# Planner costs taken from a trace, jittered filler priorities, and a later product with beta in a fused attention and gated-MLP kernel

## The chip, the core and the metric

The kernel runs on one core of a Trainium2 chip. The metric is device time in microseconds (us) of one execution, as the median of repeated runs. Below, PE is the matrix engine (TensorE; PEld is its weight load), DVE the vector engine, ACT the scalar engine, POOL the GpSimd engine, SP the engine that issues most DMAs.

## The reference

One layer over 2048 tokens of width 512 in bf16. Two branches read the same input `x`, and a gate mixes them:

```python
g = sigmoid((x * gate_w).sum(-1, keepdims=True))
a = A(x)     # attention with a compressive memory
b = B(x)     # gated MLP
return g * a + (1 - g) * b
# A: 32 heads of 16, four segments s of 512 tokens, q, k, v = x @ wq, wk, wv
p = softmax(q_s @ k_s.T * 16**-0.5 + mask)        # mask: keys up to the query
a_mem = (phi(q_s) @ M) / (phi(q_s) @ z + 1e-6)    # phi(t) = t + 1 if t > 0 else exp(t)
o_s = sigmoid(beta) * a_mem + (1 - sigmoid(beta)) * (p @ v_s)
M, z = M + phi(k_s).T @ v_s, z + phi(k_s).sum()   # then the next segment
a = o @ wo
# B: h = gelu(x @ w_gate) * (x @ w_up)  (512 -> 1792);  b = h @ w_down
```

## The kernel before

**The planner.** The kernel's body doesn't issue instructions in the order in which it is written. It describes the work as tasks (`Task`, line 43). A task has an engine or a choice of engines, a length in ns that the author states, a priority (lower goes first), dependences, and buffers that it takes and frees. Among those are the eight banks of PSUM, the memory that PE writes. `Sched.plan` (line 74) plays these tasks through in time with the stated lengths: whenever an engine is free, it starts that one of its ready tasks with the lowest priority number. The result is one fixed list, and `emit` (line 267) issues it. On the chip each engine works through its own instructions strictly in that order and waits by semaphores. The stated lengths thus never change what is computed. They set the order in which each engine gets its work, and which of two engines gets a task that either could do. If a task takes longer on the chip than stated, whatever the plan placed behind it stands and waits, even if other work would be ready.

**Stages.** First come the loads, the transposes of the first segment's `x`, and the products for k, q and v of segment 0. Then comes a gate stage: 28 tasks (`gate_pair`, line 618), each of 32 matmuls into two banks, which ACT turns into gelu and writes to `G`. Between the gate tasks of segments 0 and 1 stands one small product with `beta` (`f_bps`, line 643, priority -942). From it ACT and DVE make `omg` and `ebr`, the weights of the two attention halves; `ebr` goes into `bdeb` (`f_eb`, line 651), and `wo` is scaled by `omg` (`f_wo`, line 657). Tasks of this stage have negative priorities, so they go in the written order.

**The attention stage.** It has 80 logit slots, 20 per segment (`logit_slot`, line 694). A slot is a small PE product, two exponentials of 128x1024 on ACT (line 735), and two mask operations on POOL (line 744). PE can't be filled by these: between the slots run fillers, which `fillers` (line 1006) lists per segment, with priorities that count in slots. They are the up-projections (`up_group`, line 631, result multiplied into `G` by DVE), the q, k, v products of the next segment, the memory products (`mem_den`, `mem_num`, `m_update`), and the output products (`out_group`, line 973: down-projection and `wo` into one bank). After every five slots come two products of the probabilities with v (`pv_group`, line 752) and a chain on DVE: transpose `T` (line 781), reciprocal `r` (791), `r` times the gate (794), `N` from `T` and `r` (799), plus the memory part `Nm` (804), transpose into `xT` (807). `Nm` comes from line 952. `phi` (line 820) is one exponential on ACT, a maximum and a minimum on DVE (829, 832), and an addition on POOL (836). The output products of the last segment come at the end.

**Where the lengths stand.** `EV` (line 435) holds the default length of a task that empties a bank (`evac`, line 437); other lengths are literals in the `add` calls.

Of the kernel before, what the change touches and what calls it, by code (L numbers as in the profile page):

```python
# [1 line left out]

# [22 lines left out]
HS = DFF // P  # L25
# [8 lines left out]
SLACK = 300  # L34
NWARM = 7
NUPS = (28, 10, 9, 9)
SHAPES = {"gen": [(b,) for b in range(NBANK)],
          "pair": [(b, b + 1) for b in range(NBANK - 1)]}
WIDTH = {k: len(v[0]) for k, v in SHAPES.items()}
# [14 lines left out]
class Sched:  # L54
# [7 lines left out]
    def __init__(self, rings):  # L62
        self.tasks = []
        self.bufs = rings

    def add(self, engs, cost, fn, **kw):

        engs = {engs: cost} if isinstance(engs, str) else dict(zip(engs, cost))
        t = Task(engs, fn, **kw)
        t.seq = len(self.tasks)  # L70
        self.tasks.append(t)
        return t
# [199 lines left out]
def kernel(  # L272
# [36 lines left out]
    add = S.add  # L309
# [122 lines left out]
                **kw)  # L432
        return t, box

    EV = {"DVE": 610, "ACT": 560}

    def evac(engs, g, box, fn, prio=0.0, deps=(), alloc=(), frees=(), ring="gen", cost=None):
        engs = [engs] if isinstance(engs, str) else engs
# [29 lines left out]
    def odd_copy(s, c, ev):  # L468
        pr = c // 2
        ko = ("o", s, pr)  # L470

        def fo(e):
            if ko not in QK:
                QK[ko] = rtile("kO", [P, 2, L])
            nc.vector.tensor_scalar_mul(QK[ko][:, c % 2, :], QK[("k", s, pr)][:, c % 2, :],
                                        odd[:, :])
        new = ko not in first_ev
        o = add("DVE", 400, fo, prio=2, deps=[ev] + ([] if new else [first_ev[ko]]),
                alloc=["kO"] if new else [])
        first_ev.setdefault(ko, o)  # L480
        EVQK[("o", s, c)] = o
# [136 lines left out]
    def gate_pair(s, hp, prio):  # L618
        def mms(t):
            for i in range(2):  # L620
                mm_x(t[:, i, :], wga, (2 * hp + i) * P, s)
        g, box = group("gt", 8 * MM, mms, prio, [a_x[s], a_wg0 if hp < 2 else a_wga], alloc="pair")
        read_x[s].append(g)
        dst = G[:, s, 2 * hp:2 * hp + 2, :]
        ge = evac("ACT", g, box, lambda e, t: nc.scalar.activation(dst, t[:, :, :],  # L625
                                                                  AF.Gelu_apprx_tanh),
                  cost=960, ring="pair")
        GM[(s, hp)] = ge
        TAB["last_gt"], TAB["last_ge"] = g, ge

# [35 lines left out]
    for s in range(NSEG):  # L666
        if s == 3:
            gate_rows(-960 + 20 * s)
        for hp in range(HS // 2):
            gate_pair(s, hp, -959 + 20 * s + hp)  # L670
            if s == 0 and hp == HS // 2 - 1:
                g, box = group("bps", 60, f_bps, -942, [a_be])
                t_tb = evac("ACT", g, box, lambda e, t: nc.scalar.activation(
                    tb[:, :], t[:, 0:NCH], AF.Tanh, scale=0.5), cost=250)
                t_om = add("DVE", 100, f_omg, deps=[t_tb], prio=5)
                t_eb = add("DVE", 1200, f_eb, deps=[t_om], prio=5)
                t_wo = add("DVE", 1300, f_wo, deps=[t_om, a_wo], prio=7)
# [16 lines left out]
    def logit_slot(s, t):  # L694
# [37 lines left out]
        for h in range(2):  # L732
            def fx(_, h=h):
                pT[(s, t, h)] = rtile("pT", [P, 2, L])
                nc.scalar.activation(pT[(s, t, h)][:, :, :], A[h][:, :, :], AF.Exp, scale=0.25)  # L735

            def fa(_, h=h):
                pt = pT[(s, t, h)]
                if w in (0, 3):
                    v, pat = pt[:, :, 0:P], [[0, 2], [1, P]]  # L740
                else:
                    v = pt[:, :, :].rearrange("p h (e c) -> p (h e) c", e=2)[:, :, 0:P]
                    pat = [[0, 4], [1, P]]
                nc.gpsimd.affine_select(out=v, in_=v, pattern=pat, compare_op=ALU.is_ge,  # L744
                                        fill=0.0, base=0, channel_multiplier=-1)
            x = add("ACT", 920 + (1300 if gi == 0 and h == 0 else 0), fx, prio=1,
                    deps=[g, TAB["last_ge"]] + ([XT_[(gi, 0)]] if h else []), alloc=["pT"],
                    frees=[(("pair", h), g)])
            XT_[(gi, h)] = x
            AT[(gi, h)] = add("POOL", 380 if w in (0, 3) else 610, fa, prio=0, deps=[x])  # L750

    def pv_group(s, c, e):
        g0 = s * NSLOT + 5 * c
# [25 lines left out]

        def f_T(_, t):  # L780
            nc.vector.transpose(TT[key][:, e, :, :].rearrange("p a b -> p (a b)"), t[:, :])  # L781
        ev = evac("DVE", g, box, f_T)
        if e == 0:
            NMT[("T", key)] = g
            NMT[("Te", key)] = ev
# [20 lines left out]
        def f_o(_):  # L806
            nc.vector.transpose(xT[:, c, s * L:(s + 1) * L],
                                NN[key][:, :, :, :].rearrange("p a e d -> p (a e d)"))
        r = add("DVE", 280, f_r, prio=3, deps=[ev, NMT[("Te", key)]], alloc=["r"])
        rg = add("DVE", 120, f_rg, prio=3, deps=[r, TAB["g2"]])  # L810
        n = add("DVE", 650, f_n, prio=3, deps=[rg], alloc=["N"], frees=[("r", r), ("T", T0)])
        last = n
        if s > 0:
            last = add("DVE", 500, f_m, prio=3, deps=[n, NMT[("Nm", key)]],
                       frees=[("Nm", NMT[("Nm", key)])])
        OTT[key] = add("DVE", 640, f_o, prio=3, deps=[last] + read_x[s], frees=[("N", n)])

    PQ, PKt, PHI, PKD, RMt = {}, {}, {}, {}, {}

    def phi(src, deps, prio, mk, ring):  # L820
        box = {}

        def f_e(_):
            box["E"] = rtile("E", [P, 2, L])
            nc.scalar.activation(box["E"][:, :, :], src()[:, :, :], AF.Exp)

        def f_q(_):
            box["Q"] = rtile("Q1", [P, 2, L])
            nc.vector.tensor_scalar_max(box["Q"][:, :, :], src()[:, :, :], 0.0)

        def f_m(_):
            nc.vector.tensor_scalar_min(box["E"][:, :, :], box["E"][:, :, :], 1.0)

        def f_a(_):
            d = mk()
            nc.gpsimd.tensor_add(d[:, :, :], box["E"][:, :, :], box["Q"][:, :, :])
        e = add("ACT", 980, f_e, prio=prio, deps=deps + [TAB["first_x"], opened], alloc=["E"])
        q = add("DVE", 380, f_q, prio=5, deps=[e], alloc=["Q1"])
        m = add("DVE", 380, f_m, prio=5, deps=[e])
        return add("POOL", 2250, f_a, prio=5, deps=[m, q], alloc=[ring],  # L840
                   frees=[("E", e), ("Q1", q)])

    def phi_q(s, pr, prio):
# [22 lines left out]
    def m_update(s, pr, prio):  # L866
# [31 lines left out]
                bd[:, :, 0].rearrange("p (j e) -> p j e", j=4)[:, None, :, :]  # L898
                .to_broadcast((P, NCH, 4, 2)))
        deps = [TAB[("acc", s, 0)], acc, t_eb] + [TAB[("num", s, c)] for c in range(NCH) if s]  # L900
        TAB[("mbd", s)] = add("DVE", 620, f_mbd, prio=3, deps=deps)
        TAB[("zbd", s)] = add("DVE", 150, f_zbd, prio=3, deps=deps + ([TAB[("den", s)]] if s else []))

    def mem_den(s, prio):
        bx = {}
# [22 lines left out]
            nc.vector.tensor_mul(RMt[s][:, :, :], RMt[s][:, :, :],  # L928
                                 G2[:, s, :][:, :, None].to_broadcast((P, QB, 8)))
        ev = evac("DVE", g, box, f_T)  # L930
        a = add("DVE", 200, f_a, prio=2, deps=[ev], alloc=["rm"], frees=[("Tm", g)])
        r = add("DVE", 880, f_r, prio=2, deps=[a])
        TAB[("rm", s)] = add("DVE", 250, f_g, prio=2, deps=[r])
        TAB[("rma", s)] = a

    def mem_num(s, c, prio):
# [13 lines left out]
        def f_n(_):  # L950
# [2 lines left out]
                                 RMt[s][:, :, 2 * c:2 * c + 2][:, :, :, None]  # L953
                                 .to_broadcast((P, QB, 2, DH)))
        ev = evac("DVE", g, box, f_T)
        NMT[("Nm", (s, c))] = add("DVE", 680, f_n, prio=2.5, deps=[ev, TAB[("rm", s)]],
                                  alloc=["Nm"], frees=[("Tm", g), ("rm", TAB[("rma", s)])])

    def down(t, s, qt, lo, hi, stop):
# [13 lines left out]
    def out_group(s, qt, prio):  # L973


        late = s == NSEG - 1
        att = [t_wo] + [OTT[(s, c)] for c in range(NCH)]
        prev = first = None
        for lo in range(0, HS, 2):
            def fn(_, lo=lo):  # L980
                down(bank(first), s, qt, lo, lo + 2, False)
            prev = add("PE", 2 * MM, fn, prio=prio, mode="more" if lo else "open",
                       deps=[prev] if lo else [UPT[(s, hs)] for hs in range(HS)] + [TAB["wdn"]]
                       + ([] if late else att), alloc=[] if lo else ["gen"], final=late)
            first = first or prev
        g = add("PE", 4 * MM, lambda _: proj_o(bank(first), s, qt, range(NCH), False),
                prio=prio, deps=[prev] + att, final=late, mode="more")
        bx = {}

        def fo(e):  # L990
            bx["o"] = rtile("osb", [P, D])
            f = omz[:, s, qt:qt + 1]
            if e == "ACT":
                nc.scalar.activation(bx["o"][:, :], bank(first), AF.Copy, scale=f)  # L994
            else:
                nc.vector.tensor_scalar_mul(bx["o"][:, :], bank(first), f)  # L996
        ev = add(["DVE", "ACT"], [670, 590], fo, deps=[g, TAB["omz"]], alloc=["osb"],
                 frees=[("gen", first)])
        add("SP", 600, lambda _: store(s, qt, bx["o"]), deps=[ev], frees=[("osb", ev)], lat=2000)

# [78 lines left out]
```

## Time and profile before

| what | us |
|---|---|
| median of three runs (282.32, 282.30, 283.60) | 282.32 |
| the profiled execution, its own time | 284.42 |
| its span, first to last instruction | 282.7 |
| PE busy in the span | 272.1 |
| ACT busy | 211.3 |
| DVE busy | 173.2 |
| POOL busy | 129.1 |

The profiled execution is 1.7 us longer than its span (what lies around the program), and 2.1 us longer than the median run. Busy times are unions of recorded instructions. Records on PE, ACT and DVE overlap their successors a little: two exponentials in a row, 1025 ns each by the group's mean, take 1.94 us together, so one costs 0.92 us when ACT is kept supplied. In a window's row, each engine's busy us stands with its number of instructions in brackets, followed by the PE clock that was granted as a share of full speed, and DMA. In a row of waits stand the waiting engine and line, the one that ended the wait, and then us in total, times, and longest us.

### The profile page before, as it was taken

The page shows a single profiled execution, that of the slowest core. Times are in us where ns is not written, and L with a number is a line of the kernel's source. Part 1 is how long each engine was busy: PE and PEld are TensorE (multiplying, and loading weights), DVE is VectorE, ACT ScalarE, POOL GpSimd, SP SyncE. Part 2 cuts the span into 40 slices and gives each one's busy share as a digit, 9 for nine tenths or more (in the row PEclk, how much of TensorE's full clock was granted, in tenths as well). Part 3 has the DMA queues.
Part 4 walks back from the last instruction along what each step waited for, and adds up shares of the span by engine and source line. Part 5 has one row for each costly group of instructions (what it writes and reads, how often), then busy time and mean ns, then how long its engine had stood idle before and what let it go on. Part 6 is the DMA issues. An engine that isn't in the chain of part 4 may idle for free.

```text
span 282.7 us, 10149 instructions
## 1 busy us (share of the span) xinstructions
PE 272.1 (96%) x4498; PEld 126.6 (45%) x4504; DVE 173.2 (61%) x316; ACT 211.3 (75%) x231; POOL 129.1 (46%) x220
## 2 busy tenths in 40 slices
PE   8999899999999989999999999999999998999994
PEld 3444344444445444454445445444444443444541
DVE  2330210102879898989897797999758699535330
ACT  3545466457897777999898898898889889798520
POOL 8000000060565376486857477457645756444400
PEclk9999999999999999999999999999999998999999
DMA  7963970000022010020010020000000000000011
GB/s 237 345 125 77 339 252 2 0 0 2 3 42 39 2 39 2 2 42 2 21 39 22 3 58 23 3 2 2 21 21 22 2 21 3 21 21 21 23 38 39
DMA packets 22036, 14.02 MB, mean 50 GB/s; under 512 B 14056, under 2 KB 20968, under 8 KB 21992
## 3 DMA queue, kind: packets, MB, share of 16 engines
q1 hardware_dynamic: 21448, 12.85, 16.0%
q8 instruction: 35, 0.57, 0.9%
q10 hardware_dynamic: 544, 0.52, 0.6%
q14 instruction: 9, 0.07, 0.1%
HBM read 8.13 MB, written 2.10 MB: 36 GB/s over the span
## 4 chain that ended last, share of the span: by engine, by line
PE 74%; DVE 8%; SPq 7%; ACT 4%; DMA 2%; issue 2%; POOL 0%; ACTq 0%; DVEq 0%
PE ps L461 48%; PE ps L457 13%; PE ps L713 8%; SPq L360 7%; PE ps L763 5%; ACT pT L735 3%; DMA wdn<-in_A_x_dram 1%; DVE N L799 1%; DVE G L635 1%; DVE vz_82 L299 1%; DMA beta_76<-in_A_beta_dram 1%; DVE r L794 1%; DVE T L781 1%; DVE Nm L952 1%; DVE N L804 1%
## 5 line engine op out<-in xcount | busy, mean ns | idle before, releaser
L735 ACT ACTIVATE pT<-ps 128x1024 bf16<-128x1024 f32 x160 | 153.9, 1025 | 20.9 <-PE ps L713 20.2
L744 POOL TENSOR_SCALAR_AFFINE_SELECT pT<-pT 128x512 bf16<-128x512 bf16 (+1 forms) x160 | 92.5, 586 | 83.1 <-ACT pT L735 82.6
L461 PE MATMUL ps<-wdn,G 128*32 128x512 bf16 x896 | 59.3, 386 | 0.5 <-ACT pT L735 0.5
L461 PE MATMUL ps<-xT,wup 128*32 128x512 bf16 x896 | 55.2, 380 | 0.9 <-DVE G L635 0.8
L635 DVE TENSOR_TENSOR G<-ps,G 128x512 bf16<-128x512 f32 x56 | 37.6, 678 | 20.7 <-PE ps L461 20.3
L457 PE MATMUL ps<-xT,wga 128*128 128x512 bf16 x219 | 48.4, 379 | 0.4 <-issue 0.2
L625 ACT ACTIVATE G<-ps 128x1024 bf16<-128x1024 f32 x28 | 28.7, 1025 | 24.2 <-PE ps L457 23.5
L457 PEld LDWEIGHTS <-wga 128*128 128x128 bf16 x224 | 21.8, 98 | 26.4 <-issue 0.4
L461 PEld LDWEIGHTS <-wup 128*32 128x32 bf16 x896 | 22.3, 96 | 22.9 <-issue 4.7
L461 PEld LDWEIGHTS <-G 128*32 128x32 bf16 x896 | 21.9, 97 | 21.3 <-issue 3.9
L781 DVE STREAM_TRANSPOSE T<-ps 128x512 f32<-128x512 f32 x32 | 22.7, 708 | 13.6 <-PE ps L763 13.4
L596 POOL COPY G_87<-tt 32x16 f32<-32x16 f32 x16 | 3.1, 195 | 49.3 <-DVE tt L588 48.6
L713 PE MATMUL ps<-qT,kT 16*128 16x256 bf16 (+2 forms) x320 | 17.9, 273 | 1.5 <-DVE vz_82 L299 1.2
L713 PE MATMUL ps<-qT,kO 32*128 32x128 bf16 (+2 forms) x320 | 18.5, 276 | 0.1
L461 PEld LDWEIGHTS <-xT 128*32 128x32 bf16 x448 | 11.4, 96 | 11.3 <-issue 1.6
L461 PE MATMUL ps<-wo,xT 128*32 128x512 bf16 x256 | 16.5, 379 | 0.0
L713 PEld LDWEIGHTS <-kT 16*128 16x128 bf16 x320 | 6.9, 92 | 19.4 <-issue 19.1
L799 DVE TENSOR_TENSOR N<-T,r 128x512 bf16<-128x512 f32 x16 | 14.2, 887 | 0.4
L713 PEld LDWEIGHTS <-kO 32*128 32x128 bf16 x320 | 7.1, 93 | 14.8 <-issue 14.6
L994 ACT ACTIVATE osb<-ps,omz 128x512 bf16<-128x512 f32 x6 | 4.1, 687 | 11.5 <-PE ps L461 11.5
L996 DVE TENSOR_SCALAR osb<-ps,omz 128x512 bf16<-128x512 f32 x10 | 7.4, 743 | 8.6 <-PE ps L461 8.5
L461 PE MATMUL ps<-xT,wk 128*32 128x512 bf16 x192 | 12.5, 380 | 0.0
(116 smaller groups left out, 282.1 us busy)
## 6 DMA issues: line engine op xcount, KB each, us to landing
out_dram<-osb SPq DMA_DIRECT2D x16, 128.0 KB, 1.7
wup<-in_B_w_up_dram SPq DMA_DIRECT2D x1, 1792.0 KB, 8.1
wdn<-in_B_w_down_dram SPq DMA_DIRECT2D x1, 1792.0 KB, 13.5
wga<-in_B_w_gate_dram SPq DMA_DIRECT2D x1, 1280.0 KB, 10.3
wq<-in_A_wq_dram SPq DMA_DIRECT2D x1, 512.0 KB, 6.0
wga<-in_B_w_gate_dram SPq DMA_DIRECT2D x1, 512.0 KB
wv<-in_A_wv_dram SPq DMA_DIRECT2D x1, 512.0 KB, 7.9
wo<-in_A_wo_dram SPq DMA_DIRECT2D x1, 512.0 KB, 9.1
```

The source lines that it names most:

```text
L360: nc.sync.dma_start_transpose(xT[:, fc, s * L:(s + 1) * L], x2[s * L:(s + 1) * L, fc * P:(fc + 1) * P])
L457: nc.tensor.matmul(t, lhsT=lhsT, rhs=rhs, start=start, stop=stop)
L461: nc.tensor.matmul(t[a, :], lhsT=lhsT[:, a], rhs=rhs, start=start, stop=stop, tile_position=(0, 32 * j), skip_group_check=True)
L625: ge = evac("ACT", g, box, lambda e, t: nc.scalar.activation(dst, t[:, :, :], AF.Gelu_apprx_tanh), cost=960, ring="pair")
L635: UPT[(s, hs)] = evac("DVE", g, box, lambda e, t: nc.vector.tensor_mul(G[:, s, hs, :], t[:, :], G[:, s, hs, :]))
L713: nc.tensor.matmul(A[j // 2][:, j % 2, at * P:(at + nq) * P], lhsT=l, rhs=r, start=True, stop=True, tile_position=(32 * j, 0))
L735: nc.scalar.activation(pT[(s, t, h)][:, :, :], A[h][:, :, :], AF.Exp, scale=0.25)
L744: nc.gpsimd.affine_select(out=v, in_=v, pattern=pat, compare_op=ALU.is_ge, fill=0.0, base=0, channel_multiplier=-1)
L763: nc.tensor.matmul(t[32 * j:32 * j + 32, qb * P:(qb + nq) * P], lhsT=vz[s % 2][:, kt, h * VW:h * VW + 32], rhs=pT[(s, t0 + w, j // 2)][:, ...
L781: nc.vector.transpose(TT[key][:, e, :, :].rearrange("p a b -> p (a b)"), t[:, :])
L799: nc.vector.tensor_mul(NN[key][:, :, :, :].rearrange("p a e d -> p e a d"), TT[key][:, :, :, 0:DH], RR[key][:, :, :, :].to_broadcast((P, 2 ...
L996: nc.vector.tensor_scalar_mul(bx["o"][:, :], bank(first), f)
```

## The change

It has four parts. Nothing is computed differently.

1. 24 stated lengths are altered. The largest steps: `N` 650 to 800, `r` times gate 120 to 245, `Nm` 680 to 765, `Mbd` 620 to 825, `zbd` 150 to 335, `odd_copy` 400 to 320, the POOL addition 2250 to 2090, an ACT evacuation 560 to 495, gelu 960 to 920.
2. In `add`, every task that can only run on PE and has a priority above 0 and below 9000 gets a random number between -1.5 and 1.5 added to it, from a generator with a fixed seed. This covers all fillers. Logit slots (-10), `pv_group` (-9), the gate stage (negative) and the last segment's output products (9000 and up) are outside it.
3. The product with `beta` goes from behind the gate tasks of segment 0 to behind those of segment 1 (priority -942 to -922).
4. `out_group` waits for `att[:ATT]` with `ATT = 5`. The list `att` has five members (`t_wo` and four of `OTT`), so this is the same list.

```diff
+ATT = 5
+SEED = 7
+SPREAD = 1.5
@@ Sched.__init__, Sched.add
+        self.rng = Random(SEED)
+        if "PE" in engs and 0 < kw["prio"] < 9000:
+            kw["prio"] += self.rng.uniform(-SPREAD, SPREAD)
@@ evac's default lengths; odd_copy; gate_pair
-    EV = {"DVE": 610, "ACT": 560}
+    EV = {"DVE": 605, "ACT": 495}
-        o = add("DVE", 400, fo, prio=2, ...
+        o = add("DVE", 320, fo, prio=2, ...
-                  cost=960, ring="pair")
+                  cost=920, ring="pair")
@@ the gate stage
-            if s == 0 and hp == HS // 2 - 1:
-                g, box = group("bps", 60, f_bps, -942, [a_be])
+            if s == 1 and hp == HS // 2 - 1:
+                g, box = group("bps", 60, f_bps, -922, [a_be])
@@ logit_slot (masks), pv_group (T, r, r x gate, N, + Nm, to xT)
-            AT[(gi, h)] = add("POOL", 380 if w in (0, 3) else 610, fa, ...
+            AT[(gi, h)] = add("POOL", 400 if w in (0, 3) else 635, fa, ...
-        ev = evac("DVE", g, box, f_T)
+        ev = evac("DVE", g, box, f_T, cost=625)
-        r = add("DVE", 280, f_r, ...       rg 120   n 650   m 500   o 640
+        r = add("DVE", 260, f_r, ...       rg 245   n 800   m 490   o 610
@@ phi (e, q, m, POOL addition)
-        980, 380, 380, 2250
+        960, 330, 345, 2090
@@ m_update (Mbd, zbd), mem_den (a, r, g), mem_num (Nm)
-        620, 150;   200, 880, 250;   680
+        825, 335;   120, 860, 285;   765
@@ out_group
-                       + ([] if late else att), ...
+                       + ([] if late else att[:ATT]), ...
-        ev = add(["DVE", "ACT"], [670, 590], fo, ...
+        ev = add(["DVE", "ACT"], [660, 585], fo, ...
```

More of the change, by code (lines that the diff above doesn't have):

```diff
@@ L1 @@
 from contextlib import ExitStack
+from random import Random
 import concourse.bass as bass
@@ L477, in odd_copy @@
         new = ko not in first_ev
-        o = add("DVE", 400, fo, prio=2, deps=[ev] + ([] if new else [first_ev[ko]]),
+        o = add("DVE", 320, fo, prio=2, deps=[ev] + ([] if new else [first_ev[ko]]),
                 alloc=["kO"] if new else [])
@@ L749, in logit_slot @@
             XT_[(gi, h)] = x
-            AT[(gi, h)] = add("POOL", 380 if w in (0, 3) else 610, fa, prio=0, deps=[x])
+            AT[(gi, h)] = add("POOL", 400 if w in (0, 3) else 635, fa, prio=0, deps=[x])
     def pv_group(s, c, e):
@@ L808, in f_o @@
                                 NN[key][:, :, :, :].rearrange("p a e d -> p (a e d)"))
-        r = add("DVE", 280, f_r, prio=3, deps=[ev, NMT[("Te", key)]], alloc=["r"])
-        rg = add("DVE", 120, f_rg, prio=3, deps=[r, TAB["g2"]])
-        n = add("DVE", 650, f_n, prio=3, deps=[rg], alloc=["N"], frees=[("r", r), ("T", T0)])
+        r = add("DVE", 260, f_r, prio=3, deps=[ev, NMT[("Te", key)]], alloc=["r"])
+        rg = add("DVE", 245, f_rg, prio=3, deps=[r, TAB["g2"]])
+        n = add("DVE", 800, f_n, prio=3, deps=[rg], alloc=["N"], frees=[("r", r), ("T", T0)])
         last = n
         if s > 0:
-            last = add("DVE", 500, f_m, prio=3, deps=[n, NMT[("Nm", key)]],
+            last = add("DVE", 490, f_m, prio=3, deps=[n, NMT[("Nm", key)]],
                        frees=[("Nm", NMT[("Nm", key)])])
-        OTT[key] = add("DVE", 640, f_o, prio=3, deps=[last] + read_x[s], frees=[("N", n)])
+        OTT[key] = add("DVE", 610, f_o, prio=3, deps=[last] + read_x[s], frees=[("N", n)])
     PQ, PKt, PHI, PKD, RMt = {}, {}, {}, {}, {}
@@ L836, in f_a @@
             nc.gpsimd.tensor_add(d[:, :, :], box["E"][:, :, :], box["Q"][:, :, :])
[L837 to L840, printed above, removed]
+        e = add("ACT", 960, f_e, prio=prio, deps=deps + [TAB["first_x"], opened], alloc=["E"])
+        q = add("DVE", 330, f_q, prio=5, deps=[e], alloc=["Q1"])
+        m = add("DVE", 345, f_m, prio=5, deps=[e])
+        return add("POOL", 2090, f_a, prio=5, deps=[m, q], alloc=[ring],
                    frees=[("E", e), ("Q1", q)])
@@ L900, in m_update @@
         deps = [TAB[("acc", s, 0)], acc, t_eb] + [TAB[("num", s, c)] for c in range(NCH) if s]
-        TAB[("mbd", s)] = add("DVE", 620, f_mbd, prio=3, deps=deps)
-        TAB[("zbd", s)] = add("DVE", 150, f_zbd, prio=3, deps=deps + ([TAB[("den", s)]] if s else []))
+        TAB[("mbd", s)] = add("DVE", 825, f_mbd, prio=3, deps=deps)
+        TAB[("zbd", s)] = add("DVE", 335, f_zbd, prio=3, deps=deps + ([TAB[("den", s)]] if s else []))
     def mem_den(s, prio):
@@ L930, in mem_den @@
         ev = evac("DVE", g, box, f_T)
-        a = add("DVE", 200, f_a, prio=2, deps=[ev], alloc=["rm"], frees=[("Tm", g)])
-        r = add("DVE", 880, f_r, prio=2, deps=[a])
-        TAB[("rm", s)] = add("DVE", 250, f_g, prio=2, deps=[r])
+        a = add("DVE", 120, f_a, prio=2, deps=[ev], alloc=["rm"], frees=[("Tm", g)])
+        r = add("DVE", 860, f_r, prio=2, deps=[a])
+        TAB[("rm", s)] = add("DVE", 285, f_g, prio=2, deps=[r])
         TAB[("rma", s)] = a
@@ L955, in mem_num @@
         ev = evac("DVE", g, box, f_T)
-        NMT[("Nm", (s, c))] = add("DVE", 680, f_n, prio=2.5, deps=[ev, TAB[("rm", s)]],
+        NMT[("Nm", (s, c))] = add("DVE", 765, f_n, prio=2.5, deps=[ev, TAB[("rm", s)]],
                                   alloc=["Nm"], frees=[("Tm", g), ("rm", TAB[("rma", s)])])
@@ L983, in out_group @@
                        deps=[prev] if lo else [UPT[(s, hs)] for hs in range(HS)] + [TAB["wdn"]]
-                       + ([] if late else att), alloc=[] if lo else ["gen"], final=late)
+                       + ([] if late else att[:ATT]), alloc=[] if lo else ["gen"], final=late)
             first = first or prev
@@ L996, in fo @@
                 nc.vector.tensor_scalar_mul(bx["o"][:, :], bank(first), f)
-        ev = add(["DVE", "ACT"], [670, 590], fo, deps=[g, TAB["omz"]], alloc=["osb"],
+        ev = add(["DVE", "ACT"], [660, 585], fo, deps=[g, TAB["omz"]], alloc=["osb"],
                  frees=[("gen", first)])
```

## The prediction

> **What bounds the kernel.** I first read the busy shares, then the busy time by stage, then PE's waits, then the stretches around them. PE is busy in 96% of the span, and in the attention stage (some 66 to 263 us) in all but a few us. What is left to win is therefore PE's idle time, not any engine's load.
>
> ```profile
> PE 272.1 (96%) x4498; PEld 126.6 (45%) x4504; DVE 173.2 (61%) x316; ACT 211.3 (75%) x231; POOL 129.1 (46%) x220
> ```
> ```profile
> 90.00:120.00 30.00, 28.81 (x588) 13.59 (x584) 26.28 (x46) 23.90 (x27) 15.71 (x23) 1.00 0.05 11
> ...
> 150.00:180.00 30.00, 29.19 (x632) 13.90 (x624) 25.04 (x44) 25.52 (x29) 18.36 (x28) 1.00 0.09 25
> ...
> 210.00:240.00 30.00, 28.85 (x548) 13.16 (x548) 24.91 (x44) 27.84 (x30) 18.22 (x29) 0.97 0.04 12
> 240.00:263.00 23.00, 23.00 (x453) 10.29 (x449) 11.80 (x20) 19.27 (x22) 11.28 (x20) 0.96 0.06 21
> ```
>
> In each of these rows the first busy time is PE's. From 60 to 240 us the windows leave PE idle 4.24 us. Two numbers stand against PE's true speed: the clock in the last two rows, and the ends of matmuls, which are modelled and lie after the moment the next one could start. At 166.54 us eight matmuls start, four at a time with 0.216 us between the fours, so the next should start at 166.97; it starts at 167.79. That is 0.82 us lost where the profile shows 0.63 idle. So each wait costs about 0.19 us more than its idle time. PE has nine waits over 0.15 us in the attention stage (1.19, 0.33, 0.63, 0.17, 0.34, 0.23, 0.16, 0.33, 0.53, in all 3.91); with 9 x 0.19 = 1.71 they cost **5.6 us**. The page's own list names the releasers:
>
> ```profile
> PE ps L713 <- DVE vz_82 L299: 1.2, 1, 1.2
> PE ps L461 <- ACT pT L735: 0.9, 2, 0.5
> PE ps L461 <- DVE G L635: 0.8, 2, 0.6
> PE ps L644 <- DMA beta_76<-in_A_beta_dram: 0.7, 1, 0.7
> ```
>
> Most are DVE, although DVE is busy in only 61% of the span: it is late in places. These places are of two kinds, and they matter differently for the change.
>
> The first kind, four waits (1.19, 0.33, 0.63, 0.17; with 4 x 0.19, **3.1 us**), follows a DVE operation that took several times its usual length:
>
> ```profile
> 100.09 2.13 POOL L836 TENSOR_TENSOR pkT<-E,Q_1317 128x1024 bf16<-128x1024 bf16 x1
> 100.20 2.57 DVE L799 TENSOR_TENSOR N<-T,r 128x512 bf16<-128x512 f32 x1
> ...
> 102.69 0.68 DVE L299 CAST vz_82<-ps 128x512 bf16<-128x512 f32 x1
> ...
> 103.42 0.27 PE L713 MATMUL ps<-qT,kT 16*128 16x256 bf16 x1 [1.19 <-DVE vz_82 L299]
> ```
>
> `N` starts 0.1 us after a POOL addition, ends 0.55 us after it, and so takes 2.57 us instead of 0.68 (its length at 183.42 us). The same happens to `Nm` at 138.25 (1.53 us beside an addition from 137.10) and to `r` times gate at 164.92 (1.36 us beside one from 164.10); behind each, PE waits. That is three of the twelve additions.
>
> The second kind, five waits (0.34, 0.23, 0.16, 0.33, 0.53; with 5 x 0.19, **2.5 us**), lies where DVE works almost without a gap for many us (176 to 191, 223 to 241) and is behind its plan:
>
> ```profile
> 233.60 0.71 DVE L948 STREAM_TRANSPOSE Tm<-ps 128x512 f32<-128x512 f32 x1
> ...
> 234.36 0.73 PE L763 MATMUL ps<-pT,vz_82 128*32 128x512 bf16 x20 [0.16 <-DVE Tm L948]
> ...
> 235.64 0.28 PE L713 MATMUL ps<-qT,kT 16*128 16x256 bf16 x2 [0.33 <-ACT pT L735]
> ...
> 237.47 0.61 PE L461 MATMUL ps<-wdn,G 128*32 128x512 bf16 x8 [0.53 <-ACT pT L735]
> ```
>
> **The change part by part. beta.** The reader sees PE stand 0.68 us for beta's load before line 644. The gate matmuls around it follow each other every 0.216 us, and the next was ready. From the start of the last gate matmul before it, the small product is 0.84 us later than that pitch; some 0.09 of it I leave as the price of the detour itself (the product's own pitch). Moved behind segment 1's gates it comes some 12 us later (seven tasks of 1.72 us), long after beta has landed at 29.5. Its followers are one ACT and some ten DVE operations, with DVE idle there; `bdeb` is needed at 104.35 us and `wo` (still waiting for its own load now) at 140.65. No DMA moves. So **-0.75 us**, all on the path, since from here to 66 us PE is the path. If the cover failed the price would be the same 0.75.
>
> **Lengths.** A row's mean less the overlap of some 0.08 us is what DVE really spends when supplied (two `G` in a row of 0.68 take 1.28 together). The new numbers are just that:
>
> ```profile
> L799 DVE TENSOR_TENSOR N<-T,r 128x512 bf16<-128x512 f32 x16 | 14.2, 887 | 0.4
> ...
> L952 DVE TENSOR_TENSOR Nm<-Tm,rm 128x512 bf16<-128x512 f32 x12 | 10.2, 851 | 0.1
> ...
> L794 DVE TENSOR_TENSOR r<-r,G_87 128x32 f32<-128x32 f32 x16 | 5.3, 331 | 0.3
> ```
>
> 887, 851 and 331 become 800, 765 and 245. One chain after `pv` was stated -20 +125 +150 -10 -30 + 2 x 15 = 245 ns too short, with its `Nm` (+85) 330 ns. In a DVE stretch with three such chains the plan is 1 us ahead of the chip, about the waits of the second kind. In the other direction ACT's tasks become 65 ns (evacuation) and 40 ns (gelu) shorter, `odd_copy` 80, and POOL's addition 160, its masks 20 to 25 longer. Over the whole kernel DVE's stated work grows by about 3 us (16 x 275 for `r` times gate and `N`, 12 x 85, 3 x 390, 32 x 15, less 16 x 80, 12 x 85 and the small ones), which is no load on the chip, only a truer plan. The instructions and their lengths stay. I expect such a plan to clear 70% of the second kind: **-1.8 us**. Bounds: 0 and -2.5.
>
> For the first kind the table and a rule disagree. Read as a row, 887 is `N`'s length and the plan with 800 has room. The Trainium skill, "SBUF — State Buffer", section "Who interferes with whom", says that a DVE instruction with two SBUF inputs contends with a GpSimd instruction that reads SBUF, and that the later of the two blocks for the other's whole length. The trace agrees (2.57 us beside 2.13), so 887 is a mean of undisturbed operations and a few disturbed ones, and no stated mean can plan for a block of 1.9 us. By the row, 70% of 5.6 would go: 282.3 - 0.75 - 3.9 = 277.6. By the rule only the second kind goes: 282.3 - 0.75 - 1.8 = 279.8. I take the rule, with a small gain, since the extra 0.1 us per operation is slack and the three hits are drawn anew: **-0.6 us** (bounds +3.1, three more hits, and -3.1, none).
>
> **Priorities.** A shift of 1.5 slots, at (263 - 66)/80 = 2.5 us a slot, moves a filler by under 4 us. Products for the next segment stand eight slots ahead of need, and neighbours among the up-projections are 0.57 slots apart, so it is a reshuffle without a sign: **0**, bounds -1 and +1.5 (about the largest single wait). `ATT` is no change: 0.
>
> **Clock.** In the profiled execution PE ran at half speed from about 238 to 242 us:
>
> ```profile
> 238.00:240.00 2.00, 2.00 (x28) 0.93 (x23) 1.97 (x4) 2.00 (x3) 1.46 (x3) 0.57 0.00 0
> 240.00:242.00 2.00, 2.00 (x40) 0.78 (x36) 1.33 (x3) 0.83 (x2) 0.77 (x1) 0.58 0.00 0
> ```
>
> That is 2 x 0.43 + 2 x 0.42 = 1.7 us lost. The Trainium skill, "TensorE: Matmul & The Clock Gate", section "Why this matters for your kernels", says to avoid idle gaps over some 3 us; by it the gaps here, 0.53 at most, could not do this and the change couldn't cure it. The row stands right behind the cluster of three gaps (234.4 to 237.5), so I take it for a result of them. Against the profiled execution the sum is 284.42 - 0.75 - 1.8 - 0.6 - 1.7 = 279.6 (281.3 if the clock drop stays). The median run is 2.1 us below the profiled one, as if it mostly hadn't the drop; that can't be seen. From the median: 282.32 - 0.75 - 1.8 - 0.6 = 279.2. I forecast **279.3**.
>
> **Rivals.** *All stalls go* (0.16): the hits fall where PE doesn't wait; 282.3 - 0.75 - 5.6 = 276.0. For it: hits fall on PE's path in only three of twelve additions. *The plan is not what limits* (0.16): waits go elsewhere, since DVE is full for 15 us in places whatever the order, and only beta's gain stays: 281.6. For it: 26.3 of 30 us DVE busy in 90 to 120. *Slower* (0.06): additions meet DVE's two-input operations more often. A hit costs 3.1 / 3 = 1.0 us; the sure 0.75 and the 1.8 are eaten by 2.5 more hits, and it is slower by 0.5% from four more, seven of twelve: 282.3 - 2.55 + 4.1 = 283.9. Against it: DVE's two-input operations are no denser than before. My own case has the remaining 0.62 and spans 277.8 to 280.8.
>
> **How the numbers follow.** About 0.5%, 1.4 us, is what a measurement of this kernel can tell from no change: faster is under 280.9, slower over 283.7. Faster: 0.62 + 0.16 = 0.78; same 0.16; slower 0.06. The range takes in most of the all-go case and the beta-only case: 276.2 to 281.9.
>
> **What would show it.** beta: no wait at line 644, and the last gate task ends 0.75 us earlier. Lengths: PE's waits for DVE and ACT where no POOL addition runs sum to under 1 us. Hits: two to four DVE operations over 1.3 us, each beside line 836, each with a PE wait behind it. Clock: 1.00 through 240 us. I am wrong if waits of the second kind remain near 1.6 us of idle time, or if PE's time changes with no change in its waits.

## The result and the profile after

The changed kernel takes 279.95 us (median of four runs, 279.47 to 280.15) against 282.96 us for the kernel before, measured beside it (282.3 to 283.9). The ratio is 0.9889, 95% interval 0.985 to 0.9927. The profiled execution took 279.47 us with a span of 277.8 us; before it was 284.42 and 282.7. In the changed file, lines after the inserted ones lie seven lines lower (the DVE product with `G`, line 635 before, is line 642).

Busy shares first, as before:

```profile
PE 269.3 (97%) x4498; PEld 126.4 (46%) x4504; DVE 170.9 (62%) x306; ACT 215.6 (78%) x241; POOL 130.8 (47%) x220
```

Ten bank evacuations moved from DVE to ACT (306 and 241 instructions, before 316 and 231). The stages that were shown of before, in the same columns (us of the window, then PE busy; the PE clock is third from the end):

```profile
90.00:120.00 30.00, 28.91 (x596) 14.04 (x588) 26.14 (x44) 27.01 (x32) 17.35 (x25) 1.00 0.05 11
...
150.00:180.00 30.00, 28.95 (x592) 13.65 (x596) 26.68 (x46) 25.89 (x30) 20.57 (x26) 1.00 0.11 28
...
210.00:240.00 30.00, 30.00 (x620) 14.07 (x616) 22.59 (x41) 27.98 (x31) 17.46 (x29) 1.00 0.05 16
240.00:263.00 23.00, 22.87 (x468) 10.65 (x464) 15.89 (x25) 21.34 (x24) 13.45 (x22) 1.00 0.06 19
```

From 210 to 240 us PE has no idle time any more (1.15 us before) and the clock is full. From 90 to 120 and from 150 to 180 next to nothing is won (PE idle 1.09 and 1.05 us, before 1.19 and 0.81). PE's waits after the start of the program:

```profile
PE ps L770 <- DVE qT L306: 0.7, 1, 0.7
PE ps L720 <- DVE G L642: 0.7, 2, 0.3
PE ps L468 <- DVE Tm L925: 0.4, 1, 0.4
PE ps L770 <- DVE Tm L955: 0.3, 1, 0.3
```

The wait for beta's load is gone from the list. What remains is DVE. From the starts and ends of PE's rows in the two timelines, the 4.9 us between the spans divide as follows:

| stretch | before | after | difference |
|---|---|---|---|
| program start to first k product | 6.27 | 5.64 | -0.63 |
| to the first logit slot | 60.82 | 60.10 | -0.72 |
| to the end of the last matmul | 211.64 | 208.05 | -3.59 |
| to the end of the span | 3.97 | 3.99 | 0.0 |

The first row is no effect of the change: the code up to there is alike, and this start lay anywhere from 5.5 to 6.3 us in the executions profiled here. The second is beta. In the third, 1.7 us is the clock drop that the profiled execution of before had. The rest, 1.9 us, is fewer waits: PE's idle time from 60 to 263 us fell from 4.22 to 2.83 us, with seven waits over 0.15 us instead of nine.

Beside the first four experiments the kernel before had this clock drop (a mean clock of 0.992 to 0.994) in 26 of 43 runs, with a median of 284.04 us against 282.54 us in the other 17, so below, where two kernels are compared without a ratio, it is by the runs without the drop (for the kernel before 282.3 to 282.7 us beside each set of experiments; the changed kernel's four runs are all of this kind).

### The profile page after: what moved, and what is told of

It is laid out like the page before. It is cut to its first block, busy times and chain, and to the rows that moved or that the text cites. A ratio compares the mean times of both kernels' runs of the same rounds, so it can differ in the third digit from the quotient of the medians.

```text
span 277.8 us, 10134 instructions
## 1 busy us (share of the span) xinstructions
PE 269.3 (97%) x4498; PEld 126.4 (46%) x4504; DVE 170.9 (62%) x306; ACT 215.6 (78%) x241; POOL 130.8 (47%) x220
## 4 chain that ended last, share of the span: by engine, by line
PE 84%; DVE 11%; issue 2%; ACT 2%; ACTq 0%; DVEq 0%
PE ps L468 47%; PE ps L464 20%; PE ps L720 8%; PE ps L770 6%; DVE G L642 2%; PE ps L551 1%; DVE r L801 1%; DVE T L788 1%; PE ps L518 1%; DVE N L806 1%; ACT pT L742 1%; DVE rm L932 1%; DVE qT L306 1%; DVE xT L814 1%; ACT osb L1001 0%
## 5 line engine op out<-in xcount | busy, mean ns | idle before, releaser
L751 POOL TENSOR_SCALAR_AFFINE_SELECT pT<-pT 128x512 bf16<-128x512 bf16 (+1 forms) x160 | 94.6, 600 | 81.1 <-ACT pT L742 80.7
L642 DVE TENSOR_TENSOR G<-ps,G 128x512 bf16<-128x512 f32 x56 | 38.3, 685 | 25.4 <-PE ps L468 25.1
L632 ACT ACTIVATE G<-ps 128x1024 bf16<-128x1024 f32 x28 | 28.7, 1024 | 23.5 <-PE ps L464 22.8
L468 PEld LDWEIGHTS <-G 128*32 128x32 bf16 x896 | 21.1, 96 | 19.8 <-issue 4.1
L720 PE MATMUL ps<-qT,kT 16*128 16x256 bf16 (+2 forms) x320 | 17.3, 274 | 0.0
L1001 ACT ACTIVATE osb<-ps,omz 128x512 bf16<-128x512 f32 x11 | 7.6, 689 | 10.6 <-issue 7.0
L806 DVE TENSOR_TENSOR N<-T,r 128x512 bf16<-128x512 f32 x16 | 12.7, 793 | 0.3
L468 PE MATMUL ps<-xT,wq 128*32 128x512 bf16 x192 | 12.5, 380 | 0.1
```

What stands on the lines that cost most here:

```text
L468: nc.tensor.matmul(t[a, :], lhsT=lhsT[:, a], rhs=rhs, start=start, stop=stop, tile_position=(0, 32 * j), skip_group_check=True)
L642: UPT[(s, hs)] = evac("DVE", g, box, lambda e, t: nc.vector.tensor_mul(G[:, s, hs, :], t[:, :], G[:, s, hs, :]))
L720: nc.tensor.matmul(A[j // 2][:, j % 2, at * P:(at + nq) * P], lhsT=l, rhs=r, start=True, stop=True, tile_position=(32 * j, 0))
L806: nc.vector.tensor_mul(NN[key][:, :, :, :].rearrange("p a e d -> p e a d"), TT[key][:, :, :, 0:DH], RR[key][:, :, :, :].to_broadcast((P, 2 ...
```

## The experiments

**The parts alone.** Only the beta product moved:

```diff
-            if s == 0 and hp == HS // 2 - 1:
-                g, box = group("bps", 60, f_bps, -942, [a_be])
+            if s == 1 and hp == HS // 2 - 1:
+                g, box = group("bps", 60, f_bps, -922, [a_be])
```

> The kernel before with only the product with beta moved behind segment 1's gates. My theory: the wait at the beta product goes and nothing else moves, 0.7 to 0.8 us less than the kernel before, with the same waits of PE in the attention stage (3.9 us of idle time in nine waits). Rival (the gain is given back later, since the attention stage waits for DVE anyway): under 0.3 us.

Measured: 281.93 us, ratio 0.9959 (0.9941 to 0.9976). Without the clock drop 281.73 against 282.54, with it 283.17 against 284.04: 0.8 us either way. The nine waits of the attention stage came back one by one, the same to within 0.01 us in length, 1.4 us earlier: a fixed order has fixed waits. The whole step reached the end. The wait itself is not so fixed: where the product stood in its old place it was 0.68, 0.43, 0.62 and 1.56 us in four profiled executions, so the 0.8 us is a median's.

Only the random shift (seed 7):

```diff
+        if "PE" in engs and 0 < kw["prio"] < 9000:
+            kw["prio"] += self.rng.uniform(-SPREAD, SPREAD)
```

> The kernel before with only the random shift of the fillers' priorities (seed 7). My theory: a reshuffle without a sign, between 1 us faster and 1.5 us slower than before. Rival (the seed is where the gain is): 2 us faster or more, with beta's wait still there.

Measured: 282.15 us, ratio 0.9959 (0.9942 to 0.9976), and no run with the clock drop. Against 282.54 the gain is 0.4 us. PE's idle time from 60 to 263 us rose to 5.12 us (before 4.22), with a wait of 1.5 us for DVE at 193 us. More idle time and yet no more time: what an order costs is not all in PE's recorded gaps.

Only the new lengths, which is the changed kernel with

```diff
-SPREAD = 1.5
+SPREAD = 0.0
-            if s == 1 and hp == HS // 2 - 1:
-                g, box = group("bps", 60, f_bps, -922, [a_be])
+            if s == 0 and hp == HS // 2 - 1:
+                g, box = group("bps", 60, f_bps, -942, [a_be])
```

> The kernel before with only the new stated lengths (shift of priorities 0, beta in its old place). My theory: 1.5 to 2.5 us faster than before; PE's waits behind a full DVE without a POOL addition go from 1.6 us of idle time to under 0.6. Rival (the lengths only reshuffle, as any edit of the plan does): within 1 us of before, or slower, with as many such waits elsewhere.

Measured: 280.96 us, ratio 0.9914 (0.9882 to 0.9946), 1.6 us below 282.54. So the lengths alone bring the larger part of the gain. Idle time is 3.32 us; the cluster of three waits around 235 us is gone, though single waits appear at other places. They aren't of the kind that I expected to stay. Only one DVE operation that an addition held up has a wait of PE behind it (line 811 is `N` plus `Nm`; its median in the kernel before is 0.59 us):

```profile
192.92 2.56 POOL L843 TENSOR_TENSOR pq<-E,Q 128x1024 bf16<-128x1024 bf16 x1
194.03 1.74 DVE L811 TENSOR_TENSOR N<-N,Nm 128x512 bf16<-128x512 bf16 x1
...
196.45 1.05 PE L468 MATMUL ps<-xT,wk 128*32 128x512 bf16 x16 [0.80 <-DVE T L788]
```

The six other waits (0.22, 0.20, 0.28, 0.52, 0.35, 0.46) follow no such operation and come to 2.03 us; before they were 1.59. So the expectation of under 0.6 us failed, though the time came as expected: here the gain is in the waits behind blocks, 0.80 us instead of 2.32.

The changed kernel without the shift (`SPREAD = 0.0` alone):

> The changed kernel with the random shift set to 0 (new lengths and the later beta product stay). My theory: within 1 us of the changed kernel, so 2 to 3 us faster than before. Rival (the seed is where the gain is): 281.5 us or more, that is only beta's 0.75 us and no more.

Measured: 280.12 us, ratio 0.989 (0.9858 to 0.9922): the time of the changed kernel. For this seed the shift is worth nothing on top of the lengths. I took this for a sign that the shift doesn't matter, and that fell next.

**Other seeds.** The changed kernel with `SEED = 1`, and then with `SEED = 2`:

> The changed kernel with another seed (1 for 7). My theory: the random shift is a reshuffle without a sign, so within 1 us of the changed kernel's 280 either way. Rival (seed 7 is special): over 1.5 us slower than the changed kernel.

Measured: 284.14 us, ratio 1.0036 (1.0014 to 1.0058). Without the clock drop, which 8 of its 20 runs had, it is 283.37 us, 3.4 us slower than with seed 7, so my theory failed. Its list of PE's waits:

```profile
PE ps L468 <- DVE Macc L891: 1.5, 1, 1.5
...
PE ps L720 <- ACT pT L742: 1.0, 3, 0.5
PE ps L468 <- ACT pT L742: 0.9, 2, 0.5
PE ps L720 <- DVE Macc L891: 0.8, 1, 0.8
```

Both waits for `Macc` stand behind DVE operations blocked by a POOL addition (2.13 and 1.53 us), and a cluster of five waits from 228 to 237 us has come back.

> The changed kernel with seed 2. Seed 1 gave 284.1 us with three blocks on PE's path and a new cluster of waits from 228 to 237 us, so my theory is now that the shift draws anew where the blocks fall and where DVE is late: between 278 and 285 us, with a time that follows the number of waits of PE (each block on its path about 1 us). Rival (seed 1 is an outlier and the shift is worth nothing): 279.5 to 280.5 us.

Measured: 278.44 us, ratio 0.9847 (0.9801 to 0.9892). Idle time from 60 to 263 us is 0.99 us. So seed 7 isn't special either. Seeds 1, 7, 2 and no shift give 283.4, 280.0, 278.4 and 280.1 us: the shift has no sign, but its size is up to 3.3 us, beyond my bounds.

**The blocks.** These kernels change how phi's addition is done. First, in halves:

```diff
-            nc.gpsimd.tensor_add(d[:, :, :], box["E"][:, :, :], box["Q"][:, :, :])
+            for i in range(2):
+                nc.gpsimd.tensor_add(d[:, i, :], box["E"][:, i, :], box["Q"][:, i, :])
```

> The changed kernel with each POOL addition of phi written as two of half the size (128x512 each), which the plan still holds for one task. My theory (a DVE operation with two SBUF inputs stands until the running addition ends): the longest block halves to some 1.1 us, no DVE operation of this kind takes over 1.9 us, and PE's waits behind such blocks fall by half, 0.5 to 1.3 us less than the changed kernel. Rival (the blocks are not the addition's, or the second half follows the first with no room between): DVE operations of 2 us again, and the same time within 0.3 us.

Measured: 278.79 us, ratio 0.9845 (0.9801 to 0.9888), 1.2 us below the changed kernel, in the upper part of what I expected. The same place in the two timelines, first of the changed kernel:

```profile
110.73 2.13 POOL L843 TENSOR_TENSOR pkT<-E,Q_1632 128x1024 bf16<-128x1024 bf16 x1
110.75 2.17 DVE L801 TENSOR_TENSOR r<-r,G_87 128x32 f32<-128x32 f32 x1
...
112.95 1.05 DVE L806 TENSOR_TENSOR N<-T,r 128x512 bf16<-128x512 f32 x1
```

and then with halves:

```profile
111.04 2.27 POOL L844 TENSOR_TENSOR pkT<-E,Q 128x512 bf16<-128x512 bf16 x2
111.10 1.15 DVE L801 TENSOR_TENSOR r<-r,G 128x32 f32<-128x32 f32 x1
112.28 1.58 DVE L806 TENSOR_TENSOR N<-T,r 128x512 bf16<-128x512 f32 x1
```

`r` times gate now ends with the first half, after 1.15 instead of 2.17 us. `N` then meets the second half: DVE gets in between the two, and pays again.

Second, in place of the addition (but for 8 columns, so that the order of waits stays) POOL writes a constant and reads nothing; phi isn't computed:

```diff
-            nc.gpsimd.tensor_add(d[:, :, :], box["E"][:, :, :], box["Q"][:, :, :])
+            nc.gpsimd.tensor_add(d[:, :, 0:8], box["E"][:, :, 0:8], box["Q"][:, :, 0:8])
+            for _ in range(2):
+                nc.gpsimd.memset(d[:, :, 8:], 1.0)
```

> The changed kernel with phi's addition left out but for 8 of 512 columns; in place of the rest POOL writes a constant twice into the same tile, which takes nearly as long and reads nothing, so phi's values are not computed. My theory: no DVE operation stands beside line 843's place any more (none over 1.2 us), PE's waits behind the blocks go, and the time falls by 1.5 to 3 us against the changed kernel. Rival (DVE is full there anyway, and the blocks only fill time in which it would be late): less than 0.5 us.

Measured: 276.61 us, ratio 0.9763 (0.9718 to 0.9808), 3.3 us below the changed kernel, a little more than I expected. POOL is held as long (0.22 + 2 x 0.94 = 2.1 us), yet all of PE's waits after the start are

```profile
PE ps L468 <- DVE T L788: 0.2, 1, 0.2
PE ps L464 <- issue: 0.2, 1, 0.2
```

The same in the kernel before:

> The same replacement in the kernel before (phi's values are not computed). My theory: the four waits behind the blocks go (3.1 us by my reading of the trace), the others (beta, and those behind a full DVE from 176 to 241 us) stay, so 2 to 3.5 us less than before. Rival (all waits come from the same full DVE): under 1 us less.

Measured: 280.11 us, ratio 0.9898 (0.9839 to 0.9957); without the clock drop 279.29 (two of four runs) against 282.57, 3.3 us. The four waits behind blocks are gone, and the five others of the attention stage are there to within 0.02 us:

```profile
PE ps L461 <- ACT pT L735: 0.9, 2, 0.5
PE ps L713 <- ACT pT L735: 0.3, 1, 0.3
PE ps L461 <- DVE T L781: 0.2, 1, 0.2
PE ps L763 <- DVE Tm L950: 0.2, 1, 0.2
```

So the two kinds of waits are separate, as read, and the first kind costs what the waits' sum said (3.1).

In quarters:

```diff
+            for i in range(2):
+                for j in (0, L // 2):
+                    nc.gpsimd.tensor_add(d[:, i, j:j + L // 2], box["E"][:, i, j:j + L // 2],
+                                         box["Q"][:, i, j:j + L // 2])
```

> The changed kernel with each POOL addition of phi as four of a quarter (128x256 each). My theory (a DVE operation stands until the running addition ends, halves gave 1.2 us): blocks of at most some 0.6 us, 278.0 to 278.6 us. Rival (POOL's cost per instruction eats it, or DVE meets one quarter after another): 278.8 us or more.

Measured: 278.57 us, ratio 0.9844 (0.9805 to 0.9882). That is the time of the halves within the scatter: blocks are down to some 0.5 us each, but one chain meets several, and a quarter takes 0.67 us, so POOL works longer in all. The time lies inside my range, but only 0.2 us from the rival's, so it doesn't tell the two apart.

On DVE, with the minimum:

```diff
-            nc.gpsimd.tensor_add(d[:, :, :], box["E"][:, :, :], box["Q"][:, :, :])
+            nc.vector.scalar_tensor_tensor(d[:, :, :], box["E"][:, :, :], 1.0, box["Q"][:, :, :],
+                                           op0=ALU.min, op1=ALU.add)
-        m = add("DVE", 345, f_m, prio=5, deps=[e])
-        return add("POOL", 2090, f_a, prio=5, deps=[m, q], alloc=[ring],
+        return add("DVE", 1060, f_a, prio=5, deps=[q], alloc=[ring],
```

> The changed kernel with phi's minimum and addition as one DVE operation (stated 1060 ns) and none on POOL; phi's values are the same. My theory: no blocks by additions, as with the constant writes (276.6 us), but 12 x 0.7 us more of DVE work, some of it where DVE is full: 277 to 279 us. Rival (DVE full is what PE waits for, so any work added there costs its whole length): 281 us or more.

Measured: 278.28 us, ratio 0.9831 (0.9794 to 0.9869), the lowest median of the kernels that compute the reference (runs of 277.8 to 278.33 us; with seed 2 they are 278.02 to 278.93). The operation took 1.25 us, more than the 1.06 I had stated, and two waits of 0.5 us for ACT stand at 231 us. Against the constant writes, twelve such operations, 15 us of DVE time, cost 1.7 us. But this kernel has another plan: eight evacuations went back from ACT to DVE (314 and 233 instructions), so its order is new, and a new order alone moved the time by up to 3.3 us above. Halves, quarters and constant writes keep the plan.

**The same seed with the old lengths.** The kernel before with beta moved and the shift with seed 2 (and so, against the run with seed 2 above, with `EV = {"DVE": 610, "ACT": 560}`, `N` 650, `r` times gate 120 and the other old lengths):

> The kernel before with beta moved and the shift with seed 2, but the old lengths: against the run with seed 2 and the new lengths (278.44 us) it differs in the lengths alone. My theory (truer lengths are worth about 1.5 to 2.5 us in the mean, with a scatter of 2 us from one order to another): slower than 278.44 by 0.5 to 4 us, with more of PE's waits. Rival (the new lengths were one more lucky order, and are worth nothing in the mean): as likely below 278.4 us as above; at or below 278.4 it would speak for the rival.

Measured: 285.73 us, ratio 1.0088 (1.0062 to 1.0114), 7.3 us slower than with the new lengths, and more than I expected. From 60 to 263 us PE idles 6.76 us instead of 0.99, as the two rows show, first with the old lengths, then with the new:

```profile
60.00:263.00 203.00, 196.24 (x3919) 92.19 (x3921) 160.50 (x273) 173.98 (x193) 114.83 (x169) 1.00 0.08 18
```
```profile
60.00:263.00 203.00, 202.01 (x4050) 94.42 (x4053) 155.92 (x280) 176.89 (x193) 116.51 (x175) 1.00 0.08 18
```

Most of this is blocks again. With the old lengths the three longest DVE operations of the attention stage are

```profile
96.17 2.53 DVE L897 TENSOR_TENSOR Mbd<-Macc,bdeb 128x512 bf16<-128x512 f32 x1
193.75 2.35 DVE L810 TENSOR_TENSOR N<-N,Nm 128x512 bf16<-128x512 bf16 x1
227.28 2.08 DVE L805 TENSOR_TENSOR N<-T,r 128x512 bf16<-128x512 f32 x1
```

each beside an addition (96.02, 193.70, 226.68 us), with PE waits of 1.04, 1.37, and 1.05 and 0.31 us behind them. With the new lengths only one operation takes over 1.2 us (1.78), and PE has no wait behind it.

There are thus three pairs that differ in the lengths alone, or for seed 7 in the lengths and beta: no shift 281.73 to 280.12; seed 7 282.15, less 0.8 for beta, to 279.95; seed 2 285.73 to 278.44. The new lengths are better in each, by 1.6, 1.4 and 7.3 us. That is shown for these three orders; if the lengths did no more than draw a new order, as likely worse as better, three of three would still come up one time in eight. The size in the mean isn't shown, with three draws of such scatter.

The waits don't account for all of it, either: with seed 2 PE idles 0.99 us and with the constant writes 0.73, and yet these two kernels are 1.8 us apart.

## Why the prediction was right, point by point

The forecast was 279.3 us with a range of 276.2 to 281.9; measured were 279.95 us. The likeliest case, "waits of the second kind go, those of the first stay", is the one that came. The parts add up: 0.8 for beta, 1.6 for the lengths, 0.2 for the shift. But luck has a share in it. The change fixes one seed, and with seed 1 the same change took 283.4 us, outside the range and slower than before; and whether the lengths gain by the first or by the second kind of wait differs from order to order.

- **beta, -0.75.** Right in size and in reaching the end: 0.8 us alone, 0.72 in the trace. It was read from one execution, whose wait happened to be near the usual one.
- **Lengths, -1.8 from waits of the second kind.** Right in size, and in the changed kernel right in kind: the waits that stand behind no addition are 0.17 and 0.23 us of idle time; with my 0.19 each that is 0.8 us, before 2.5. But the lengths alone, worth the same 1.6 us, didn't bring this kind down at all: there the second kind costs 3.2 us (six waits) and the first 1.0 (one wait), before 2.5 and 3.1. Seed 7 turned this round again. Between its two kernels, old lengths and new, the idle time of the second kind fell from 2.6 to 0.40 us, and that of the first hardly moved (2.2 and 2.05); between those with seed 2 it was mostly the first that fell. So no kind of wait can be called the one that the lengths act on.

  Nor was "only a truer plan" right. My new numbers were means, less the overlap of 0.08 us. In the rows by line, the shortest, the median and the longest of each operation stand behind the colon, in ns:

```profile
L799 DVE TENSOR_TENSOR N<-T,r x16: 680/693/2570, 86.5 to 269.0; 128x512 bf16<-128x512 f32 x16
L794 DVE TENSOR_TENSOR r<-r,G_87 x16: 174/192/1361, 86.3 to 268.8; 128x32 f32<-128x32 f32 x16
```

  Less 0.08, the usual `N` takes 0.61 us and the usual `r` times gate 0.11. The old 650 and 120 were nearer to that than the new 800 and 245, and for `Nm` (median 774) the old 680 was nearer than 765. So an undisturbed chain wasn't stated 245 ns too short; the new plan leaves room in it. Whether this room, the shorter ACT and POOL tasks or simply another order made the gain stays open. Moved evacuations don't explain it: ten went from DVE to ACT in the changed kernel, three with the lengths alone, and in the pair with seed 2 four went the other way.
- **Blocks by the addition, -0.6.** The mechanism was right, the gain was not there. After the change five waits (0.34, 0.68, 0.33, 0.37, 0.33) follow three blocked operations beside additions at 110.73, 124.07 and 164.38 us: 2.05 + 5 x 0.19 = 3.0 us, before 3.1. So the term was about 0, and the step "the extra 0.1 us per operation is slack" is not borne out in this order. With the lengths alone the same term was about -2.1; that the hits are drawn anew was the part that held, and its bounds of 3.1 us either way were the honest size. The runs with constant writes put the price of all blocks at 3.3 us in both kernels. Between the profile's row and the Trainium skill's rule ("SBUF — State Buffer", "Who interferes with whom") the rule was the one to take for what a block is, as halves and constant writes show; that the sum came so near to the rule's 279.8 us and not to the row's 277.6 is in part the draw.
- **Priorities, 0 with bounds -1 and +1.5.** The value was right for seed 7 (-0.2 on top of the rest), by the luck of the seed, and the bounds were wrong: against no shift, +3.3 us with seed 1 and -1.7 with seed 2. I had bounded it by the largest single wait; an order has many waits, and a new order draws all of them, the blocks' places included.
- **Clock.** The profiled execution of the changed kernel has clock 1.00 throughout, and my 279.6 against that execution stands beside 279.47. That the drop comes from the cluster of short gaps, where the Trainium skill ("TensorE: Matmul & The Clock Gate", "Why this matters for your kernels") warns of gaps over some 3 us, is only argued: the kernels whose profile has a cluster of three or more waits between 228 and 238 us (before, beta alone, constant writes in before, seed 1) had the drop in part of their runs, and none of the others had it. Among those others are kernels with two waits there (0.87 and 0.19 us with the shift alone; 1.05 and 0.31 with seed 2 and the old lengths). How little PE works there doesn't decide it: from 234 to 238 us it was busy 2.90 us before and 2.92 with the shift alone, in whose 22 runs the clock never dropped. No run takes the cluster away by itself, so the cause stays open.

Of the signs that I had named, beta's wait is gone, the waits beside no addition are 0.40 us in all (under 1 us), and the clock is full through 240 us; of DVE operations over 1.3 us there is one (2.17 us) and not two to four, with two more of 1.20 and 1.21, each with PE's waits behind it. With the lengths alone the sign against me would have shown: the second kind stood at 2.03 us.

The rival "the plan is not what limits" is refuted by the orders themselves: with the same work they spread from 278.4 to 285.7 us. "All stalls go" is refuted by the blocks that stayed. "Slower", by more blocks, is what seed 1 is in small part (2.8 us of idle time behind them, before 2.3); its other waits grew more, to 2.7.

## What to carry to other kernels

When lengths for a fixed order are taken from a trace, look at the median and the longest beside the mean: here the mean mixed operations that another engine held up with those that it didn't, and described neither. No run here tests whether medians plan better. A tie-breaking change in such an order is no small edit; its time must be measured over several draws before a gain is put down to anything else in the same change, and that holds for changed lengths too, since they also draw a new order. And a long two-input operation on GpSimd beside a busy VectorE can cost more than its own length shows: halves of it, in the same plan, gave 1.2 us here. A fused operation on VectorE gave 1.7, with a new order in it.

## What had not been expected of the hardware

- The clock: half speed for some 3.4 us (1.7 us lost) at 238 us, behind three waits of 0.16, 0.33 and 0.53 us within 4 us, and again behind the same three in the run with beta alone:

```profile
234.00:236.00 2.00, 1.22 (x10) 0.39 (x10) 2.00 (x4) 2.00 (x4) 1.39 (x2) 1.00 0.00 0
236.00:238.00 2.00, 1.89 (x20) 0.87 (x23) 1.76 (x5) 2.00 (x4) 1.59 (x3) 0.52 0.00 0
238.00:240.00 2.00, 2.00 (x35) 0.74 (x24) 1.97 (x4) 0.81 (x1) 1.23 (x3) 0.63 0.00 0
```

  It happened in 26 of 43 runs of the kernel before, whose median was 1.5 us higher (284.04 against 282.54).
- DVE operations with one SBUF tensor input stood beside the addition too: `odd_copy`, 0.35 us alone, took 1.40 us with seed 1 (at 103.02 us, beside the addition from 102.13), and the addition of 1e-6 in `mem_den` 1.20 us instead of 0.23 in the changed kernel (at 125.08 us, beside the addition from 124.07).
- POOL's masks hold DVE up as well, for less long: in the kernel before, `N` took 1.16 and 1.17 us where it started with a mask (at 86.53 and 246.84 us, masks from 86.51 and 246.83), against its median of 0.69. Such stretched operations are in the means too, and the constant writes don't remove them.
- POOL's addition takes 2.13, 1.16 and 0.67 us for 1024, 512 and 256 columns, so by these three a part of some 0.2 us doesn't shrink.
